# A decode step of attention and a gated MLP: fifteen loads of a few bytes behind the last weights

## The chip, the cores and the metric

The kernel runs on one core of a Trainium2 chip. The metric is the time of one execution on the device in microseconds (us). The core's engines are TensorE (PE in the profile, its weight loads PEld), VectorE (DVE), ScalarE (ACT), GpSimd (POOL) and SyncE (SP). Each has its own stream of instructions, and they meet through semaphores. Data moves between the chip's memory (HBM) and the core's SBUF by sixteen DMA engines, which take their work from queues that SP and ScalarE fill.

## The reference

One token is taken through two blocks, and a gate mixes their results.

```python
x = A_x                                        # [1, 1, 1024]
g = sigmoid((x * gate_w).sum(-1))
# A: grouped attention, 32 query heads, 4 key/value heads of 128, 65536 cached keys
q = x @ wq                                     # wq [1024, 4096]
p = softmax(q . k_cache * 128 ** -0.5)         # k_cache, v_cache [1, 4, 65536, 128]
a = (p . v_cache) @ wo                         # wo [4096, 1024]
# B: a gated MLP with a norm in its second half
z = gelu(x @ w_in)                             # w_in [1024, 3584]
b = (z1 * (w_sp * layernorm(z2) + b_sp)) @ w_out
out = g * a + (1 - g) * b                      # [1, 1, 1024]
```

All inputs and the output are in bfloat16. Nearly all the work is reading: the two caches and the weights come to 162.01 MB, and each byte is used once.

## The kernel before

The kernel holds one large SBUF tensor, `arena`, which it cuts by hand into named regions (a list of names and sizes, placed one behind the other). The largest is `RING`, five slots into which all large loads go. PSUM holds the scores (`scp`), the attention output (`obt`), a small scratch (`mbt`) and the final sum (`fbt`).

The order of the work is written out by hand at the end of the kernel function. `k_step` handles one block of 16384 keys of one head: four VectorE transposes (L499), each followed by TensorE products into `scp` (the helper `mm`, L261 and L263). Blocks go in pairs. After a pair `score_pair` takes the scores to SBUF, `exp_pair` makes their exponentials on ScalarE, and `pv_piece` multiplies a block of values into `obt`. Block B is worked in between, near the start. At the end come the attention's output weights `wo`: `wo_rows` for its first half, then `wo_piece` (L717) for the third quarter and for the last quarter in three cuts of 5, 2 and 1 chunks (`WO_CUT`), all added up in `fbt`. VectorE copies `fbt` to `orow` (L778), and `store` sends `orow` to the output from SP (L365).

Every operation goes through a small recorder, `R.op` (called `P`), which is told the engine, the keys that the operation reads and those that it writes. From these keys `plan` works out which semaphores an operation waits for, and `emit` writes out each engine's instructions in the order in which they were recorded, the waits ahead of them. A load counts up a semaphore of its own name (`dma=`) by 16 when it has landed. At the very end SP waits until the store has landed (L122).

All large loads stand in a list, `stream`, in the order in which they are to be issued, and all leave from SP's queue. `issue` (L386) records as many of them as it can: it stops at the first load whose place in the ring still holds data that isn't marked as used. `done(key)` marks a block as used and calls `issue` again. So the loads' order on SP is that of `stream`, and each waits for the engine that frees its place. The last five are the pieces of `wo`: 4 MB, 2 MB, and the cuts of 1280, 512 and 256 KB. Behind them SP has only the store. Four small loads at the start (`small`, L288) leave from ScalarE's queue: two of eight rows of 256 bytes, two of one element of 2 bytes.

Of the kernel before, what the change touches and what calls it, by code (L numbers as in the profile page):

```python
# [138 lines left out]
def bass_gated_mix__gqa_block_cached__mixer_gmlp__decode_kernel(  # L139
# [23 lines left out]
    FC = FH // 128  # L163
# [12 lines left out]
    QW = DO // NW  # L176
# [11 lines left out]
    def region(name, nbf):  # L188
        nonlocal cur
        OFF[name] = cur  # L190
        cur += (nbf + 15) // 16 * 16

    for name, n in [
        ("M16", 32), ("MQ", 32),
        ("RING", NSUB * SUB), ("KT", NKT * 4096), ("SC", NSC * 2048), ("PSB", 2 * 1024), ("PTSB", 2 * 1024),
        ("QPAD", 4 * QP), ("IDB", 128), ("BM", 256), ("SEL", 16 * 32),
        ("XT", KC), ("WB", 2), ("WBB", 4), ("ONEB", 128),
        ("MAXC", 2 * total), ("LP", 2 * total), ("COLS", 2 * 64), ("DM", 64), ("ONES", 256), ("QALL", 128), ("OVZ", 32 * OC + 31), ("E4Z", 128), ("MHALF", 4),
        ("YB", FC), ("OROW", QW),
    ]:  # L200
        region(name, n)
    NA = (cur + 63) // 64 * 64
# [2 lines left out]
    def ab(name, n, o=0):  # L205
        return arena[:, OFF[name] + o:OFF[name] + o + n]
# [4 lines left out]
    def vw(base, off, dims, p0=0, np_=128):  # L211
        ps = base.ap[0][0]
        return bass.AP(tensor=base.tensor, offset=base.offset + off + p0 * ps,
                       ap=[[ps, np_]] + [list(d) for d in dims])
# [7 lines left out]
    yb, ovz, orow = ab("YB", FC), ab("OVZ", 32 * OC + 31), ab("OROW", QW)  # L222
# [33 lines left out]
    P = R.op  # L256
# [45 lines left out]
    stream = []  # L302
# [58 lines left out]

    osrc = orow[W0:W0 + NW, :]

    def store():
        P("SP", lambda e: e.dma_start(out[0, 0].rearrange("(q n) -> q n", n=QW), osrc), r=["orow"],  # L365
          w=["out"], dma="out")

    issued = [0]
    used = set()
# [2 lines left out]
    def grains(off, w):  # L372
        return list(range(off // GRAN, (off + w + GRAN - 1) // GRAN))

    def issue():

        while issued[0] < len(stream):
            n = issued[0]
            keys, off, src = stream[n]
            w = src.shape[1]  # L380
            gr = grains(off, w)
            if any(k not in used for x in gr if x in owner for k in owner[x]):
                return
            for j, x in enumerate(gr):
                owner[x] = (keys[j * len(keys) // len(gr)],)
            P("SP", lambda e, o=OFF["RING"] + off, w=w, src=src: e.dma_start(arena[:, o:o + w], src),  # L386
              w=[("slot", x) for x in gr], dma="s%d" % gr[0])
            issued[0] += 1

    def use(key):  # L390
        n, off, w = place[key]
        assert n < issued[0], key
        return arena[:, OFF["RING"] + off:OFF["RING"] + off + w], [("slot", x) for x in grains(off, w)]

    def done(key):
        used.add(key)
        issue()

    issue()


# [8 lines left out]
      r=["m32"], w=["sel"])  # L410
    P("DVE", lambda e: e.tensor_reduce(mq, vw(idf, 0, [[1, 16], [16, 8]]), AXX, ALU.add), r=["idf"], w=["mq"])
    P("DVE", lambda e: e.tensor_reduce(mhalf, vw(idf, 0, [[32, 2], [64, 2], [1, 32]]), mybir.AxisListType.XY, ALU.add),
      r=["idf"], w=["mhalf"])
# [4 lines left out]
    for fe in range(4):  # L418
        P("POOL", lambda e, fe=fe: e.tensor_copy(vw(sele, 128 * fe, [[32, 4], [1, 32]]),
                                                vw(idb, 64 * (fe // 2) + fe % 2, [[0, 4], [2, 32]])),  # L420
          r=["idb"], w=[KSE])
# [5 lines left out]
    def f(e):  # L427
        for c in range(KC):
            ins = e.matmul(tb[:, c:c + 1], vw(xm, c, [[8, 128]], 0, 8), oneb[0:8, 0:1], start=(c == 0),  # L429
                           stop=(c == KC - 1), skip_group_check=True)  # L430
        return ins
# [3 lines left out]
      r=["oneb", "wsp", "bsp"], w=["mb"])  # L435
# [6 lines left out]
      r=["ones", "gs"], w=[KTB])  # L442
# [4 lines left out]
      r=["g"], w=["omg"])  # L447
# [328 lines left out]
    for c0, c1 in WO_CUT:  # L776
        wo_piece(3, c0, c1)
    P("DVE", lambda e: e.tensor_copy(orow[0:W0 + NW, :], fb[0:W0 + NW, 0:QW]), w=["orow", "fb"])  # L778
    store()

    R.ahead = 2
# [30 lines left out]
```

## Time and profile before

| what | value |
|---|---|
| time, median of 3 runs | 380.72 us (380.72 to 380.83) |
| span of the profiled execution, first to last instruction | 379.6 us |
| read from HBM | 162.01 MB, 427 GB/s over the span |
| DMA queue q1 (SP's loads and the store) | 3616 packets, 98.9% of sixteen engines |
| DMA queue q10 (ScalarE's small loads) | 36 packets |
| DMA queue q8 (instructions) | 9 packets, 0.15 MB |
| PE busy | 229.6 us (60%) |
| DVE busy | 204.7 us (54%) |
| ACT busy | 23.3 us (6%) |

The profile describes one execution. Its span runs from the first to the last instruction, and all moments in it are counted from the span's start. The three timed runs measure a little more than the span, since they hold what lies around it; the page gives no other time for the profiled execution. "Idle before" and waits name what released an engine, inferred from semaphores. The trace also holds every packet of the DMA engines with its start, its duration, its size and its queue, but not the number of the engine that carried it. A DMA engine's row of packets can be followed where one packet begins as the one before it ends.

### The profile page before, as it was taken

What the parts mean: (1) busy time and instruction counts of PE and PEld (TensorE: products, weight loads), DVE (VectorE), ACT (ScalarE), POOL (GpSimd) and SP (SyncE); (2) the same over time, 40 slices, a digit from 0 to 9 for tenths busy, and PEclk for the clock granted to TensorE, in tenths of its full rate; (3) what the DMA queues carried; (4) which work ended last, traced back from release to release, by engine and by line L of the source; (5) the groups of instructions that cost most, each with busy time, mean ns of one, the idle gap of its engine ahead of it and who ended that gap; (6) DMA issues with size and microseconds to landing.
All of it is one profiled execution on the core that took longest, in us unless ns stands there. A gap on an engine that the chain in (4) does not pass through costs nothing.

```text
span 379.6 us, 2565 instructions
## 1 busy us (share of the span) xinstructions
PE 229.6 (60%) x1444; PEld 57.4 (15%) x835; DVE 204.7 (54%) x162; ACT 23.3 (6%) x24; POOL 8.2 (2%) x36
## 2 busy tenths in 40 slices
PE   0061488458558923895389428952896199737296
PEld 0010011011111200122012001220111011211024
DVE  4011496778389524974597248745773387412021
ACT  1000000010420000002200000022000000220000
POOL 5000000000000000000000000000000000000000
PEclk9997599696859985998599859995799589958599
DMA  9999999999999999999999999999999999999996
GB/s 442 421 414 394 483 388 439 439 453 391 437 442 442 442 430 435 435 442 442 442 430 394 421 442 442 444 435 428 435 435 437 435 442 442 430 421 414 418 428 263
DMA packets 3662, 162.17 MB, mean 427 GB/s; under 512 B 452, under 2 KB 452, under 8 KB 708
## 3 DMA queue, kind: packets, MB, share of 16 engines
q1 hardware_dynamic: 3616, 162.01, 98.9%
q8 instruction: 9, 0.15, 0.1%
q10 hardware_dynamic: 36, 0.00, 0.0%
q14 instruction: 1, 0.01, 0.0%
HBM read 162.01 MB, written 0.00 MB: 427 GB/s over the span
## 4 chain that ended last, share of the span: by engine, by line
DMA 68%; PE 16%; DVE 14%; ACT 1%; issue 1%; ACTq 0%; SPq 0%
DMA arena<-in_A_k_cache_dram 47%; DVE arena L499 12%; DMA arena<-in_A_wo_dram 8%; DMA arena<-in_A_v_cache_dram 7%; PE scp L261 6%; PE scp L263 5%; DMA arena<-in_B_b_sp_dram 5%; PE obt L261 2%; PE obt L263 2%; DVE arena L536 1%; PE fbt L717 1%; ACT arena L531 1%; ACTq L288 0%; PE fbt L665 0%; ACT arena L661 0%
## 5 line engine op out<-in xcount | busy, mean ns | idle before, releaser
L499 DVE STREAM_TRANSPOSE arena<-arena 128x2048 f32<-128x2048 f32 x64 | 143.0, 2284 | 56.7 <-DMA arena<-in_A_k_cache_dram 41.8
L261 PE MATMUL scp<-arena 128*128 128x512 bf16 (+1 forms) x274 | 111.5, 423 | 95.7 <-DVE arena L499 95.4
L263 PE MATMUL scp<-arena 128*128 128x512 bf16 (+1 forms) x275 | 110.4, 418 | 0.0
L261 PE MATMUL obt<-arena 128*64 128x512 bf16 (+2 forms) x334 | 61.4, 410 | 14.2 <-DMA arena<-in_A_v_cache_dram 14.2
L263 PE MATMUL obt<-arena 128*64 128x512 bf16 (+2 forms) x334 | 61.0, 408 | 0.0
L261 PEld LDWEIGHTS scp<-arena 128*128 128x128 bf16 (+1 forms) x274 | 27.4, 104 | 206.6 <-issue 103.5
L536 DVE STREAM_TRANSPOSE arena<-arena 128x2048 bf16<-128x2048 bf16 x7 | 16.2, 2311 | 27.0 <-PE obt L263 24.8
L531 ACT ACTIVATE arena<-arena 128x2048 bf16<-128x2048 f32 x8 | 16.0, 2002 | 218.4 <-DVE arena L528 195.0
L261 PEld LDWEIGHTS obt<-arena 128*64 128x64 bf16 (+1 forms) x334 | 17.9, 111 | 65.7 <-issue 59.0
L516 DVE TENSOR_SCALAR_CACHE_REDUCE arena<-scp 128x2048 f32<-128x2048 f32 x8 | 18.3, 2291 | 16.0 <-PE scp L263 16.0
L565 DVE RECIPROCAL arena<-mbt 128x1 f32<-128x1 f32 x4 | 0.6, 139 | 17.5 <-PE mbt L560 17.5
L539 DVE STREAM_TRANSPOSE arena<-arena 128x1024 bf16<-128x1024 bf16 x2 | 2.5, 1245 | 12.9 <-PE obt L263 12.9
L487 POOL COPY arena<-arena 32x32 bf16<-32x32 bf16 x16 | 3.2, 203 | 234.4 <-PE scp L263 209.8
L434 PE MATMUL mbt<-arena 1*128 1x2 bf16 x1 | 0.2, 159 | 12.2 <-DMA arena<-in_B_b_sp_dram 12.2
L436 DVE COPY arena<-mbt 128x2 f32<-128x2 f32 x1 | 0.2, 159 | 12.2 <-PE mbt L434 12.2
L578 PE MATMUL mbt<-arena 128*64 128x128 bf16 x8 | 1.3, 313 | 7.7 <-DVE arena L572 7.7
L429 PE MATMUL scp<-arena 8*128 8x1 bf16 x8 | 0.7, 198 | 8.6 <-DVE arena L424 8.6
L717 PE MATMUL fbt<-arena 128*32 128x128 bf16 x128 | 4.1, 220 | 1.2 <-DMA arena<-in_A_wo_dram 1.2
L778 DVE CAST arena<-fbt 36x128 bf16<-36x128 f32 x1 | 0.3, 282 | 7.2 <-PE fbt L717 7.2
L528 DVE TENSOR_REDUCE arena<-mbt 128x1 f32<-128x32 f32 x4 | 0.8, 192 | 6.0 <-PE mbt L525 6.0
L717 PEld LDWEIGHTS fbt<-arena 128*32 128x32 bf16 x128 | 3.6, 97 | 2.4 <-issue 1.2
L464 DVE CAST arena<-obt 97x1024 bf16<-97x1024 f32 x1 | 1.2, 1225 | 4.8 <-PE obt L263 4.8
(92 smaller groups left out, 54.9 us busy)
## 6 DMA issues: line engine op xcount, KB each, us to landing
arena<-in_A_k_cache_dram SPq DMA_DIRECT2D x2, 4096.0 KB, 33.3
arena<-in_B_w_in_dram SPq DMA_DIRECT2D x1, 7168.0 KB, 30.5
arena<-in_A_wo_dram SPq DMA_DIRECT2D x1, 4096.0 KB, 38.3
arena<-in_B_w_out_dram SPq DMA_DIRECT2D x1, 3584.0 KB, 21.4
arena<-in_A_wo_dram SPq DMA_DIRECT2D x1, 2048.0 KB, 27.2
arena<-in_A_wo_dram SPq DMA_DIRECT2D x1, 1280.0 KB, 29.9
arena<-in_A_wo_dram SPq DMA_DIRECT2D x1, 512.0 KB, 30.7
arena<-in_A_wo_dram SPq DMA_DIRECT2D x1, 256.0 KB, 30.8
```

The costliest lines, as they stand in the source:

```text
L261: return e.matmul(*a, **kw)
L263: one = e.matmul(*a, **kw).ins
L464: P("DVE", lambda e: e.tensor_copy(psb[0:97, :], ob[0:97, :]), w=["psb", "ob"])
L487: P("POOL", lambda e, pb=pb: e.tensor_copy(vw(qpad, 24 + 32 * pb, [[QP, 4], [1, 8]], 32 * pb, 32), vw(qall, 8 * g, [[32, 4], [1, 8]], 32 * ...
L499: P("DVE", lambda e: e.transpose(ktb(i).bitcast(F32), sl[:, 4096 * p:4096 * (p + 1)].bitcast(F32)), r=keys[4 * p:4 * p + 4], w=[("kt", i % ...
L516: P("DVE", lambda e: e.tensor_scalar(scs(j), scp[:, :], 0.0, None, op0=ALU.add, op1=ALU.max, accum_out=maxc[:, j:j + 1]), w=[("sc", j % 2) ...
L528: P("DVE", lambda e: e.tensor_reduce(gcol(g, K_NB), mb[:, 0:32], AXX, ALU.min), w=[("nb", g), "mb"])
L531: P("ACT", lambda e: e.activation(psb2, scs(j), ACTF.Exp, bias=gcol(j // 2, K_NB), scale=SCALE, accum_out=lp[:, j:j + 1]), r=[("sc", j % 2 ...
L536: P("DVE", lambda e: e.transpose(ptsb2, psb2), r=["psb"], w=[("ptsb", 0), ("ptsb", 1)])
L539: P("DVE", lambda e: e.transpose(ptsb(n), ab("PSB", 1024, 1024 * (n % 2))), r=["psb"], w=[("ptsb", n % 2)])
L578: ins = e.matmul(mb[64 * g:64 * (g + 1), 0:128], vw(sel, 128 * c, [[2, 64]]), osc[:, 128 * c:128 * (c + 1)], start=(c == 0), stop=(c == 3) ...
L717: ins = e.matmul(fb[32 * b:32 * (b + 1), 0:QW], ovz[:, z:z + 32], sl[:, o:o + QW], start=False, stop=(i == 3 and c == 7), tile_position=(0 ...
```

## The change

A region `TINY` of 32 elements is added behind all others in the arena. A new function `marks` records fifteen loads on SP. The load for k (from 15 down to 1) takes k rows of two bfloat16 elements, four bytes, from the first rows of `A_wq` to as many partitions of `TINY`; each load has columns of its own. All fifteen count up one semaphore, `tiny`. `issue` calls `marks` once, right behind the last load of `stream`, which is the 256 KB cut of `wo`. The store now also names the fifteen loads among what it reads, so SP waits for their count as well before it issues the store. Nothing reads the loaded bytes.

```diff
-        ("YB", FC), ("OROW", QW),
+        ("YB", FC), ("OROW", QW), ("TINY", 32),
...
+    tiny = ab("TINY", 32)
+
+    def marks():
+        for k in range(15, 0, -1):
+            def f(e, k=k):
+                with nc.allow_non_contiguous_dma(reason="a few bytes"):
+                    return e.dma_start(tiny[0:k, 2 * k:2 * k + 2], A_wq[0:k, 2 * k:2 * k + 2])
+            P("SP", f, w=[("tiny", k)], dma="tiny")
+
     def store():
-        P("SP", lambda e: e.dma_start(out[0, 0].rearrange("(q n) -> q n", n=QW), osrc), r=["orow"],
-          w=["out"], dma="out")
+        P("SP", lambda e: e.dma_start(out[0, 0].rearrange("(q n) -> q n", n=QW), osrc),
+          r=["orow"] + [("tiny", k) for k in range(1, 16)], w=["out"], dma="out")
...
             issued[0] += 1
+            if issued[0] == len(stream):
+                marks()
```

## The prediction

> **What bounds the kernel now.** I read the page's 40 slices first (DMA at 9 tenths or more in all but the last), then its queue table (the load queue q1 holds 98.9% of sixteen DMA engines), then the last 35 us, where the change sits. The chain of waits ends like this (start us, us, what):
>
> ```profile
> 345.42 0.33 SPq L386
> 345.75 0.04 issue
> 345.79 29.93 DMA arena<-in_A_wo_dram
> 375.72 0.14 issue
> 375.86 2.16 PE fbt L717 x64
> 378.01 0.02 issue
> 378.04 0.28 DVE arena L778
> ```
>
> The reader is to see that the end is set by output weights arriving, then by four short steps. What SP does meanwhile is in its own timeline from 345 us on and in its waits:
>
> ```profile
> 345.42 1.76 SPq L386 DMA_DIRECT2D arena<-in_A_wo_dram  x4
> 378.35 0.37 SPq L365 DMA_DIRECT2D out_dram<-arena  x1
> ```
>
> ```profile
> SPq L365 <- DVE arena L778: 31.1, 1, 31.1
> SPq L386 <- PE obt L263: 14.5, 1, 14.5
> SPq L122 <- DMA out_dram<-arena: 0.8, 1, 0.8
> ```
>
> SP has issued its last weights at 347.19 (345.42 + 1.76) and then has nothing to do for 31.1 us. Last, the tail cut into stretches (us, busy and count of each engine, clock, DMA share, GB/s):
>
> ```profile
> 370.00:375.50 5.50, 4.33 (x88) 2.69 (x81) 0.68 (x2) 0.78 (x1) 0.00 (x0) 1.00 0.98 409
> 375.50:376.40 0.90, 0.54 (x20) 0.57 (x22) 0.00 (x0) 0.00 (x0) 0.00 (x0) 1.00 0.58 232
> 376.40:377.30 0.90, 0.90 (x40) 0.89 (x35) 0.00 (x0) 0.00 (x0) 0.00 (x0) 1.00 0.44 148
> 377.30:378.40 1.10, 0.70 (x20) 0.37 (x14) 0.28 (x1) 0.00 (x0) 0.00 (x0) 1.00 0.00 0
> ```
>
> Two things carry the forecast. The DMA engines don't finish together: their share falls from 0.98 to 0.58 to 0.44. And from 377.30 to 378.40 they move nothing, while TensorE, VectorE and SP bring the result to the store.
>
> The trace's packet records sharpen this. The last load (256 KB) is eight 2 KB packets on each of sixteen engines, 80 ns apart, then a 4-byte packet for the count. The sixteen engines end it between 375.50 and 377.26; seven by 375.87, nine from 376.43 on. The last count packet is over at 377.27, the weight load that waited for it starts at 377.59: **a count takes 0.32 us to be seen**. The store shows the same: its last count packet is over at 379.23, SP's wait passes at 379.57, so 0.34.
>
> **The change, part by part.** Nothing is removed or moved: on every engine but SP the built program has the same instructions in the same order. Added are fifteen loads on SP behind the last weights, and one more count to wait for ahead of the store.
>
> *SP's issuing.* The nearest rows are the four small loads on ScalarE's queue (0.57, 0.28, 0.27, 0.41 us) and SP's own issues (0.33 to 0.44, one of 1.44), with gaps of 0.04. I take 0.44, the row just ahead on the same queue: 15 x 0.48 = 7.2 us, from 347.19 to 354.4. With the shortest row it is 15 x 0.31 = 4.7 (351.9), with the longest 15 x 1.48 = 22.2 (369.4). All of it lies in SP's 31.1 us wait. Nothing is queued behind it except the store, needed at 378.35, and even the longest case is done 6 us before the first DMA engine is through with its weights (375.50). Cost 0. If the queue would not hold so many pending loads, SP would stand still in the same idle time; at 347.19 it already held five whole loads and most of a sixth, and those issues took 0.33 to 0.44.
>
> *The DMA engines.* Each engine meets its short packets after its weights, so no weight can be late by them, as long as they don't disturb engines still on weights. They don't compete visibly: 2 KB packets are 80 ns apart on the engines that end first, with all sixteen busy, and on the one that ends last, with few busy. What a short load costs the engine that carries it: behind 64 KB packets of the first load, the 2-byte data packets of the one-row loads and the 4-byte count packets each delay the next packet by 5 to 6 ns, a 256-byte row by 14. Data and count are 11 ns by these, 24 at most (18 for a recorded 256-byte packet, and 6). The eight-row loads at the start put one row on each of eight engines. If no load gives one engine more than one row, no engine gets more than 15 pairs: 15 x 11 = 0.17 us, at most 15 x 24 = 0.36. Even on the slowest engine they are through by 377.44 to 377.63, and seen 0.34 later, at 377.8 to 378.0. The store can't leave before VectorE ends at 378.32. **0.3 to 0.5 us of cover is left; cost 0.**
>
> Where the cover ends: 378.32 - 0.34 - 377.27 = 0.71 us for 15 pairs, so 47 ns a pair on the slowest engine. The one-row loads ran on one of the eight engines that took the eight-row ones. Following that engine packet by packet (each begins where the one before ends), I get its last weights at 375.65: 2.33 us of cover, 155 ns a pair. Tracks could be exchanged where they cross, so I keep 47 ns as the strict bound. If all 120 rows went to the slowest engine: 120 x 11 = 1.32 us, seen at 378.93, cost 0.6.
>
> Which engines they are is told only by the Trainium skill, DMA: Bandwidth & Descriptors, "Why a DMA increments its semaphore by 16 and not by 1": a load of k rows goes to the lowest-numbered k engines. By that rule one engine gets all fifteen and the last none; the eight packets of each eight-row load agree, and no run here numbers the engines.
>
> *The added wait.* The built program has SP wait for the loads' count first, then for VectorE. SP's separate wait at the end takes 17 ns, and this one is passed before 378.32. Cost 0; met after VectorE instead, 0.02.
>
> *Memory.* 64 bytes per partition behind everything else; no other offset moves.
>
> Sum: span 379.59 + 0. The span lies 1.13 below the median of the three runs (380.72 - 379.59), and I add that again for what lies around it: **380.7 us**.
>
> **The rivals.**
>
> *Each short load waits for the one before it (slower).* No row shows short packets straight behind one another on one engine. If a load's data had to wait until the count before it was seen, each would cost 0.34: 15 x 0.34 = 5.1 us. From 375.65 that ends at 380.75, from 377.27 at 382.37; the store leaves 2.4 to 4.0 us late: **383.1 to 384.7**. It decides from 47 ns a pair (strict bound) or 155 (the followed engine). For it: only the last store waits, so nothing else would hide it. Against it: all through the trace a count packet is followed by the next load's data after 6 ns, and in the store the count packets start 12 to 18 ns behind the data. Chance 0.12.
>
> The Trainium skill speaks for this rival: the same page, "Anatomy of one DMA", gives a DMA about 2.0 us that don't shrink with its size, most of it the receipt of the write. Fifteen of these in a row would be an estimated 30 us and some 409 in all; all side by side, the count would be seen near 379.3 and the time would be some 381.7. The trace disagrees for a store of eight rows: 0.86 us from the end of its issue (378.72) to the wait passed (379.57).
>
> *A tenth instruction fetch (slower).* The instruction queue shows nine fetches of 16 KB. Eight come before 377, and each costs its DMA engine about 1.4 us: 0.95 for itself, and the 64 KB packet beside it takes 2.9 instead of 2.42. That is about the distance between the early and the late engines. One more, on a late engine, would move the end from 377.27 to 378.7: **382.1**. For it: SP's program grows by fifteen instructions and a wait. Against: the fetches come some 45 us apart, as TensorE works through its 2,279 recorded instructions, and SP has some 40. Chance 0.03.
>
> By the Trainium skill, Runtime: NRT & Kernel Launch, "Instruction fetch mechanics", a block of 16 KiB holds 256 instructions; nine times that is 2,304, which fits TensorE's count, and SP's program is far from filling one.
>
> *The end comes earlier (faster).* The only opening is the uneven end of the engines: were the fetches dealt to other engines by the shifted issue times, the last could end with the eighth-last (376.75), -0.5: 380.2. A gain over 0.2% would need all engines level. Nothing in the change moves a fetch before 347. Chance 0.04 for more than 0.2%.
>
> *The change doesn't do what it says.* It would, if the loads left SP only after the weights had landed. Even the longest issue row (369.4) rules that out, and the time would be the same; it counts with the forecast.
>
> **How the numbers follow.** A measurement of this kernel can tell about 0.2% (0.76 us) from no change. Forecast (cover holds, or is missed by less than 0.76): 0.81. Series: 0.12. Tenth fetch: 0.03. Faster: 0.04. So slower 0.15, same 0.81, faster 0.04. The range reaches from 380.2 (fetches dealt luckily) over 381.3 (all rows on the slowest engine) to 382.1 (a tenth fetch); the series rival lies outside.
>
> **What would show it.** After the change, SP's timeline should show fifteen issues from 347.2 to about 354, and its wait for VectorE at L778 should still end last before the store. The packet records should show the 4-byte packets of an engine 5 to 25 ns apart right behind its 2 KB packets, the last by about 377.6; the stretch between last weights and store should stay near 1.1 us; the instruction queue should count nine fetches. I am wrong if the store is released by a DMA instead of VectorE, if the short packets stand 50 ns or more apart, or if the last weights land later than 377.3 against the span's start.

## The result, and the profile after

| | before | after |
|---|---|---|
| median of 6 runs | 380.72 us (380.6 to 380.83) | 381.91 us (381.79 to 382.23) |
| span of the profiled execution | 379.6 us | 380.4 us |

The ratio is 1.0031 (95% interval 1.002 to 1.0042): 1.19 us slower, 0.31%. The time lies inside the predicted range, but the forecast was no change, and this is a change.

The chain of waits of the kernel after (start us, us, what) ends as before, with the output weights, TensorE and VectorE:

```profile
344.94 0.33 SPq L395
345.27 0.04 issue
345.31 30.20 DMA arena<-in_A_wo_dram
375.51 0.14 issue
375.65 1.75 PE fbt L728 x56
377.40 0.01 issue
377.41 0.42 PE fbt L728 x8
377.83 0.02 issue
377.85 0.28 DVE arena L789
```

VectorE is done at 378.13, 0.18 us earlier than before. The chain view stops there and doesn't show the loss. SP's timeline does, and its waits give the releaser (total, times, longest):

```profile
344.94 1.76 SPq L395 DMA_DIRECT2D arena<-in_A_wo_dram  x4
346.75 13.85 SPq L370 DMA_DIRECT2D arena<-in_A_wq_dram  x15
379.20 0.29 SPq L374 DMA_DIRECT2D out_dram<-arena  x1
```

```profile
...
SPq L108 <- DMA arena<-in_A_wq_dram: 18.5, 1, 18.5
SPq L395 <- DVE arena L638: 13.6, 1, 13.6
SPq L808 <- PEq L808: 1.0, 1, 1.0
SPq L122 <- DMA out_dram<-arena: 0.9, 1, 0.9
```

The store leaves at 379.20, 1.07 us behind VectorE; before, the distance was 0.03. The wait for L778 (now L789) that closed SP's idle time is gone from the list. In its place stands a wait for the short loads (L108). The same stretches of the tail as before (us, busy and count by engine, clock, DMA share, GB/s):

```profile
370.00:375.50 5.50, 3.96 (x83) 2.69 (x81) 0.61 (x2) 0.65 (x1) 0.00 (x0) 1.00 0.96 396
375.50:376.40 0.90, 0.75 (x28) 0.79 (x30) 0.00 (x0) 0.00 (x0) 0.00 (x0) 1.00 0.60 223
376.40:377.30 0.90, 0.90 (x36) 0.82 (x30) 0.00 (x0) 0.00 (x0) 0.00 (x0) 1.00 0.38 107
377.30:378.40 1.10, 0.50 (x12) 0.23 (x8) 0.28 (x1) 0.00 (x0) 0.00 (x0) 1.00 0.00 0
378.40:379.60 1.20, 0.00 (x0) 0.00 (x0) 0.00 (x0) 0.00 (x0) 0.00 (x0) 1.00 0.00 0
```

From 377.30 until the store's own packets (379.97) no packet is on record. The last weights end at 377.03, and the last packet of a short load begins at 377.08. Packets of four bytes stand 6 ns apart behind an engine's weights, as predicted. Yet SP waits until 379.12.

Besides packets, the trace records when a count is seen. There the short loads look different. Their 120 counts are seen from 375.88 to 379.12, those of several engines mixed. One even row runs to the end among them: 378.118, 378.319, 378.520, 378.721, 378.922, 379.124. That looks like one engine's row, 0.201 us apart, and the first experiment bears it out. **An engine's packets record a short load every 12 ns, but its counts are seen 0.18 to 0.20 us apart.**

### The profile page after: what moved, and what is told of

Read it like the earlier page. It is cut to its first block, busy times and chain, and to the rows that moved or that the text cites. A ratio compares the mean times of both kernels' runs of the same rounds, so it can differ in the third digit from the quotient of the medians.

```text
span 380.4 us, 2579 instructions
## 1 busy us (share of the span) xinstructions
PE 225.3 (59%) x1442; PEld 56.8 (15%) x835; DVE 204.4 (54%) x162; ACT 23.2 (6%) x24; POOL 8.2 (2%) x36
## 4 chain that ended last, share of the span: by engine, by line
DMA 75%; DVE 12%; PE 12%; issue 0%; ACTq 0%; SPq 0%
DMA arena<-in_A_k_cache_dram 55%; DVE arena L510 11%; DMA arena<-in_A_wo_dram 8%; DMA arena<-in_A_v_cache_dram 7%; DMA arena<-in_B_b_sp_dram 5%; PE scp L261 4%; PE scp L263 4%; PE obt L261 2%; PE obt L263 1%; PE fbt L728 1%; ACTq L288 0%; SPq L395 0%; PE scp L452 0%; DVE arena L451 0%; DVE arena L789 0%
## 5 line engine op out<-in xcount | busy, mean ns | idle before, releaser
L261 PE MATMUL scp<-arena 128*128 128x512 bf16 (+1 forms) x272 | 108.9, 417 | 98.8 <-DVE arena L510 98.3
L263 PE MATMUL scp<-arena 128*128 128x512 bf16 (+1 forms) x275 | 108.7, 412 | 0.2 <-issue 0.2
L261 PE MATMUL obt<-arena 128*64 128x512 bf16 (+2 forms) x334 | 60.8, 406 | 15.1 <-DMA arena<-in_A_v_cache_dram 15.1
L263 PE MATMUL obt<-arena 128*64 128x512 bf16 (+2 forms) x334 | 60.3, 402 | 0.0
L789 DVE CAST arena<-fbt 36x128 bf16<-36x128 f32 x1 | 0.3, 282 | 7.2 <-PE fbt L728 7.2
```

Source lines behind the costliest of these rows:

```text
L261: return e.matmul(*a, **kw)
L263: one = e.matmul(*a, **kw).ins
```

## The experiments

Theory A: on one DMA engine a load's count comes 0.18 to 0.20 us behind the count before it. Its rivals: the 120 counts hold each other up on the one semaphore (B); short pieces of four bytes are dear (C); the loss is not in the wait at all. Each run was timed beside the kernel before on the same chip. Each difference in us below is between the medians of runs taken together, the ratios have 95% intervals.

**Own counts.**

```diff
-            P("SP", f, w=[("tiny", k)], dma="tiny")
+            P("SP", f, w=[("tiny", k)], dma="tiny%d" % k)
```

> The fifteen loads as in the change, but each counts up a semaphore of its own. In the changed kernel the last count packet is recorded at 377.09 us and the last count is seen at 379.12, and counts of one engine come about 0.18 to 0.20 us apart. Theory A (series on the engine: an engine's next short load is not counted until the count before it is through, 0.18 to 0.20 each, up to fifteen on one engine): nothing changes, last count near 379.1, 381.9 us. Theory B (120 counts meet on one semaphore and hold each other up): the spread goes away, last count near 377.5, 380.7 us. Fifteen own semaphores also name each count's load, so each engine's row of counts can be read off.

Measured: 382.1, ratio 1.0035 (1.0022 to 1.0047). B falls, since the rows of counts stay as they were. The trace of the change spoke against B too: six counts there are seen 8 to 9 ns apart on the one semaphore (378.064 to 378.105). And each count now has a name. The load of one row counts on one engine; that engine carries all fifteen loads. Its weights' count is seen at 375.61 and its fifteenth short count at 378.316: 15 x 0.180. The last count of all belongs to the load of six rows (378.991) and has no successor in the loads of fewer rows. So it is on an engine with ten loads, whose weights' count is seen at 377.03: 10 x 0.196. **Not the engine with the most loads ends last, but a late one with ten.** The store left at 379.35, 0.36 behind that count, because SP still went through the remaining waits, two semaphores at a time, 0.06 us apart. That part of 382.1 is the experiment's own.

**One load with fifteen pieces.**

```diff
-        for k in range(15, 0, -1):
...
+                return e.dma_start(vw(tiny, 0, [[4, 15], [1, 2]], 0, 16),
+                                   A_wq[0:16, 0:60].rearrange("p (a b) -> p a b", b=4)[:, :, 0:2])
```

> One load in place of fifteen: sixteen rows of fifteen separate pieces of four bytes, so each of the sixteen engines carries fifteen short data packets and one count (240 pieces in place of 120 rows, 16 counts in place of 120). Theory A (the price is per count in series): one more count per engine, seen about 0.2 us behind the last weights' count (377.4 to 377.6), well before VectorE is done: 380.7 us. Theory C (the price is per piece of four bytes, a short write, whatever is counted): 15 x 0.18 to 0.20 on every engine, the slowest of them too, so the last count is near 380.2, the store about 2 us late: 382.7 us.

Measured: 380.73, ratio 0.9999 (0.9991 to 1.0008). SP's timeline and waits:

```profile
344.68 1.75 SPq L394 DMA_DIRECT2D arena<-in_A_wo_dram  x4
346.47 0.43 SPq L369 DMA_DIRECT2D arena<-in_A_wq_dram  x1
378.13 0.36 SPq L373 DMA_DIRECT2D out_dram<-arena  x1
```

```profile
SPq L108 <- DMA arena<-in_A_wq_dram: 30.6, 1, 30.6
...
SPq L373 <- DVE arena L788: 0.6, 1, 0.6
```

The wait for the short load is over 0.6 us before VectorE's, which closes the idle time again. All sixteen engines carried fifteen pieces, twice as many as in the change, and their counts came 0.16 to 0.22 us behind their weights' counts (both taken in order of time), the last at 377.49. So pieces are cheap and C falls. Counts are dear.

**Rows of 512 bytes.**

```diff
-                    return e.dma_start(tiny[0:k, 2 * k:2 * k + 2], A_wq[0:k, 2 * k:2 * k + 2])
+            P("SP", lambda e, k=k: e.dma_start(ab("SC", 256, 256 * k)[0:k, :], A_wq[0:k, 256 * k:256 * k + 256]),
+              w=[("tiny", k)] + ([("sc", 0), ("sc", 1)] if k == 15 else []), dma="tiny")
```

> The fifteen loads with rows of 512 bytes in place of 4, into a part of the arena that is free by then; SP first waits for ScalarE, which was done with it 10 us before. Theory A: the same row of counts, with 14 to 20 ns more per row: up to fifteen x 0.02 = 0.3 us later, 381.9 to 382.2 us. Theory C (short writes are dear): rows of 512 bytes are cheap, last count by 377.9, 380.7 us.

Measured: 382.19, ratio 1.0038 (1.0024 to 1.0052). The row of counts that ends last is 378.406, 378.607, 378.809, 379.010, 379.211: 0.201 apart, as with four bytes. The row's bytes are not added to the step; they pass inside it.

**Waiting behind the store.**

```diff
-          r=["orow"] + [("tiny", k) for k in range(1, 16)], w=["out"], dma="out")
+          r=["orow"], w=["out"], dma="out")
...
         nc.sync.wait_ge(dsem["out"], final["out"])
+        nc.sync.wait_ge(dsem["tiny"], final["tiny"])
```

> The fifteen loads as in the change, but SP waits for them only behind its wait for the store, not ahead of the store. The store leaves right after VectorE (about 0.03 us). If the wait alone carries the loss and the queues behind it are free: 380.7 to 380.8 us. If the engine that takes all fifteen is itself held until its last count (379.1), its row of the store comes no earlier than that, and the store is through near 379.7 to 379.9: 380.8 to 381.1 us. If the loss came from somewhere else than the wait ahead of the store, it stays at 381.9.

Measured: 381.16, ratio 1.0008 (1.0 to 1.0017), 0.40 us over before. The store leaves at 378.06, 0.03 behind VectorE, as before the change. Most of the loss is therefore the wait ahead of it. Part of the rest shows in the store's eight counts: seven are seen by 379.24, the eighth at 379.432, 0.201 behind the last short load's (379.231). The store's row on that engine stands in the same line: the store's data packets are all over by 378.91. The profiled execution is one of the fastest of this kernel (380.77, against the median of 381.16), so it is not shown that these 0.2 us make up the whole 0.40.

**How many, and where.** Three kernels, in this order: only the five loads of 15 to 11 rows; fifteen loads of sixteen rows; fifteen loads of one row.

```diff
-        for k in range(15, 0, -1):
+        for k in range(15, 10, -1):
...
-          r=["orow"] + [("tiny", k) for k in range(1, 16)], w=["out"], dma="out")
+          r=["orow"] + [("tiny", k) for k in range(11, 16)], w=["out"], dma="out")
```

```diff
-                    return e.dma_start(tiny[0:k, 2 * k:2 * k + 2], A_wq[0:k, 2 * k:2 * k + 2])
+                    return e.dma_start(tiny[0:16, 2 * k:2 * k + 2], A_wq[0:16, 2 * k:2 * k + 2])
```

```diff
-                    return e.dma_start(tiny[0:k, 2 * k:2 * k + 2], A_wq[0:k, 2 * k:2 * k + 2])
+                    return e.dma_start(tiny[0:1, 2 * k:2 * k + 2], A_wq[0:1, 2 * k:2 * k + 2])
```

> Only the five loads of 15 to 11 rows. By theory A the last count is that of an engine that ends its weights late (count seen near 377.1 to 377.4 in the changed kernel) and carries five: plus 5 x 0.20 = 378.1 to 378.4; with 0.08 to the store against VectorE's 378.16 that is 0.0 to 0.3 us late: 380.7 to 381.0 us. If the loss came with having such loads at all, however many, it stays at 381.9.

> Fifteen loads of sixteen rows each, so that every engine carries fifteen, the one that ends its weights last too. Theory A: its weights' count is seen at 377.3 to 377.5, plus 15 x 0.18 to 0.20 = 2.7 to 3.0, so the last count comes at 380.0 to 380.5 and the store 1.9 to 2.4 us late: 382.6 to 383.1 us. If the sum of all counts mattered (225 + 15 in place of 120 at 27 ns each): the spread doubles from 3.2 to 6.5 us, 385 us.

> Fifteen loads of one row each. In the runs with own counts the load of one row counts on the engine that all fifteen loads have in common, and that engine ends its weights early (count seen at 375.6). Theory A: 375.6 + 15 x 0.18 = 378.3, in another run of the fetches up to 375.9 + 15 x 0.2 = 378.9; the store is 0.2 to 0.7 us late: 380.9 to 381.4 us. If the price were per load of SP's queue, whichever engine carries it: 381.9.

Measured, with the moments of each profiled execution (distances are taken before rounding):

| loads | last short count | VectorE done | store leaves | behind VectorE | time, over before | ratio |
|---|---|---|---|---|---|---|
| the change, 15 to 1 rows | 379.12 | 378.13 | 379.20 | 1.07 | 381.91, 1.19 | 1.0031 (1.002 to 1.0042) |
| five, 15 to 11 rows | 378.15 | 378.18 | 378.23 | 0.04 | 380.82, 0.11 | 1.0004 (0.9995 to 1.0012) |
| fifteen, 16 rows | 380.87 | 378.13 | 380.95 | 2.82 | 383.33, 2.62 | 1.0068 (1.0055 to 1.0081) |
| fifteen, 1 row | 378.51 | 378.11 | 378.59 | 0.47 | 381.09, 0.38 | 1.0010 (1.0001 to 1.0019) |

The loss follows the store's delay each time. With sixteen rows the latest weights' count is 377.36, and the last short count stands 3.51 behind it, more than the 2.7 to 3.0 expected, though the row that ends last has steps of 0.178 (380.333, 380.511, 380.689, 380.866). Followed back in steps of 0.17 to 0.18, its fifteen counts begin at 378.41, 1.05 us behind the latest weights' count, so the step alone doesn't explain the whole distance. An instruction fetch begins at 377.23 and lasts 2.19 us (the one at 372.05 took 0.93, the last one of the kernel before 1.48); whether it ran on that engine is not recorded, so this stays open. The sum of counts doesn't set the time: 240 counts at the change's 27 ns each would have taken 6.5 us, and they took 5.1 (375.80 to 380.87). The one-row run is the cleanest. A single engine carries everything, and its counts are seen at 375.975, 376.155, 376.335 and so on to 378.508, thirteen of the fourteen steps 0.180 or 0.181 and one 0.192. SP's own issues took as long there as in the change:

```profile
346.97 13.73 SPq L370 DMA_DIRECT2D arena<-in_A_wq_dram  x15
378.59 0.29 SPq L374 DMA_DIRECT2D out_dram<-arena  x1
```

So the price is not per load of SP's queue either.

**Ahead of the weights.** Does only the counting lag, or does the engine stand still?

```diff
-            if issued[0] == len(stream):
-                marks()
...
+            if n == len(stream) - 5:
+                marks()
```

> The same fifteen loads and the same wait, but the loads are issued ahead of the first piece of the output weights instead of behind the last, so that 8 MB of weights stand behind them on the engines. Theory A1 (only the counts of an engine come 0.18 to 0.20 us apart, its data flows on meanwhile): the fifteen counts are through some 10 us before the end, the last weights land as before (near 377.3), nothing is late: 380.7 us. Theory A2 (the engine stands still until each count is through): engine 0 loses 15 x 0.18 = 2.7 us and a late engine with ten loads 10 x 0.2 = 2.0 us of its transfer time, the last weights come 1.7 to 2.0 us later: 382.4 to 382.7 us.

Measured: 382.05, ratio 1.0038 (1.0025 to 1.0051). The short loads are through at 360.37, 19 us before the store, and the run is still 1.34 slower. One stretch of this run, and below it the same stretch of the change:

```profile
355.00:360.00 5.00, 1.83 (x10) 0.59 (x6) 0.00 (x0) 0.00 (x0) 0.00 (x0) 0.50 0.81 282
```

```profile
355.00:360.00 5.00, 1.91 (x10) 0.58 (x6) 0.00 (x0) 0.00 (x0) 0.00 (x0) 0.50 0.91 393
```

The rate there falls from 393 GB/s (419 in the kernel before) to 282. That SP issues the first piece of `wo` 6 us later (335.24 instead of 328.94) is not the reason: its first packet begins at 355.98, and at 355.90 in the change. The four-byte packets are again recorded 6 ns apart, but the first 32 KB packet behind them lasts up to 2.44 us instead of 1.21. The last weights end at 378.68 instead of 377.03 (377.26 in the kernel before), and the loss arrives through the weights:

```profile
345.17 32.02 DMA arena<-in_A_wo_dram
377.19 0.14 issue
377.33 2.18 PE fbt L728 x64
379.51 0.02 issue
379.53 0.28 DVE arena L789
```

Theory A1 (data flows on meanwhile) falls. Fifteen short loads in a row hold the engine. The size comes out below A2: 1.4 to 1.7 us in this execution, which is one of the slower ones (382.38), against 1.7 to 2.0, and a median of 382.05 against 382.4 to 382.7.

**Spread out, and on the other queue.**

```diff
-    def marks():
-        for k in range(15, 0, -1):
+    def marks(k0=15, k1=0):
+        for k in range(k0, k1, -1):
...
-            if issued[0] == len(stream):
-                marks()
+            if 3 <= issued[0] < 18:
+                marks(18 - issued[0], 17 - issued[0])
```

> The same fifteen loads on SP's queue, but one behind each of fifteen large loads from the third on, instead of all at one place. The run ahead of the weights showed that fifteen in a row hold the engine: the first 32 KB packet behind them lasted up to 2.4 us instead of 1.21, and the last weights came 1.4 to 1.7 us late. Theory H1 (each count holds its engine 0.18 to 0.20 us, wherever it stands): an engine that carries ten loses 2.0, one that carries fifteen 2.7, and the end comes 1.4 to 2.0 us later: 382.1 to 382.7 us. Theory H2 (an engine reads on while one count is pending, and only several in a row stop it): a single one is hidden in the large packets around it: 380.7 to 380.9 us.

```diff
-            P("SP", f, w=[("tiny", k)], dma="tiny")
+            P("ACT", f, w=[("tiny", k)], dma="tiny")
```

> The fifteen loads as in the change, issued by ScalarE instead of SP, from about 337 us on, when it has nothing else to do for 32 us. The four small loads at the start of the kernel show how the two queues share an engine: one packet from one, one from the other, so data and count of a short load each follow one large packet (2.42 us for 64 KB, 0.61 for 16 KB). Thirty packets are through by about 375, ahead of the last weights. H1 (each count holds the engine 0.18 to 0.20): 1.4 to 2.0 us late, 382.1 to 382.7 us. H2 (hidden between large packets): 380.7 to 380.9 us.

Measured: spread 381.24, ratio 1.0012 (1.0003 to 1.0021), 0.56 over before; other queue 380.9, ratio 1.0004 (0.9995 to 1.0013), 0.22 over. Spread out, the last weights end at 377.52, 0.26 us later than before; on the other queue at 376.97, and the last short count is seen at 372.22. H1 (every count holds its engine 0.18 to 0.20) falls in both. H2 fits the other queue and comes out low for the spread loads: between large packets most of the price is hidden, not all. What the 0.56 us of the spread loads is made of stays open; the 0.22 us of the other queue can't be told from no change.

## Why the prediction was wrong, point by point

That 381.91 lies inside the range is luck. The range reached up to 382.1 only for a tenth instruction fetch, which did not come, and the rival that came closest to the mechanism stood outside it. Of the three signs of being wrong that the prediction named, one came: a DMA's count releases the store, not VectorE.

- **SP's issuing: no cost, as predicted, though longer.** 13.85 us instead of 7.2, inside the bounds of 4.7 and 22.2. The first ten took 0.30 to 0.48 each and the last five 1.07 to 2.63. That fits a queue that would not hold so many loads, which the prediction had considered, and it cost nothing, as the working said. With one row and with sixteen rows a load the eleventh is again the first long one (1.01 and 1.57 us), so the sum of rows is not what fills it.
- **The weights: undisturbed, as predicted.** They end at 377.03, against 377.26 before.
- **The price of a pair: the step that failed.** "Data and count are 11 ns by these, 24 at most." The 5 to 6 ns were taken from how little a short packet delays the record of the next packet, behind 64 KB packets. The packets after the change stand 6 ns apart too, so the row was read rightly, but for the wrong quantity. SP waits for counts, and those come 0.18 to 0.20 us apart. The term of 15 x 11 ns = 0.17 us, at most 0.36, was in fact 2.7 us on the engine with all fifteen (15 x 0.180) and 2.0 on the one that ended last (10 x 0.201). The prediction had noted that no row shows short packets straight behind one another, and its upper bound still came from packets alone; the 0.32 us until a count is seen belonged into that bound, not only into a rival.
- **Where the cover ends: right, and it decided.** 47 ns a pair on the slowest engine, 155 on the one that carries all fifteen. Measured 180 exceeds both. For the engine with all fifteen, 15 x 0.18 = 2.7 against 2.33 us of cover leaves 0.37 us, and the run with one row lost 0.38. So close a match is partly chance, since in that run's own profile the store was 0.47 us behind VectorE. In the change a late engine with ten loads (ten as in the run with own counts) overtook it: 377.1 + 10 x 0.201 = 379.1.
- **The series rival: the mechanism, at half its price.** It took 0.34 a load and 15 loads (383.1 to 384.7). The runs show 0.18 to 0.20 and ten loads on the engine that ends last. Its contrary evidence, a count packet followed by data after 6 ns, was again taken from packet records, which don't show the hold: ahead of the weights, packets recorded 6 ns apart went with 2.44 us in place of 1.21 for the next large one.
- **The 2.0 us by the Trainium skill** (DMA: Bandwidth & Descriptors, "Anatomy of one DMA"). That section is written for DMAs that GpSimd issues, and these are issued by SP. The estimate from it with all loads side by side (some 381.7) lies near the 381.91 measured, but not by its mechanism: a fixed price would not have gone with five loads (0.11 us) nor risen with sixteen rows (2.62 us).
- **The lowest-numbered engines.** The own counts agree with the rule that the prediction took from the Trainium skill (same page, "Why a DMA increments its semaphore by 16 and not by 1"): the loads have 15, 14, 13 and so on to 1 counts, and the engine that has the one-row load's count has one of each. No run numbers the engines.
- **The tenth fetch** did not come: the instruction queue counts nine in both. **The added wait** cost 0.08 us from the last count to the store's issue, where the prediction had 0.02 for a wait met after VectorE.

The Trainium skill, DMA: Bandwidth & Descriptors, "Queues, rings and completion order", says that a count lands only after every earlier write of its engine. The series agrees with that order; the section gives no time for it. What an engine does in the 0.18 us was not tried and stays open; no run separates the count from the write just ahead of it.

## What to carry to other kernels

The price of short loads in a row at the end of a kernel is the step from count to count on an engine, in these runs 0.18 to 0.20 us a load, and not the few nanoseconds that their packets take: one load of fifteen pieces was free where fifteen loads cost 1.2 us. Where several small loads stand behind one another, make them one, or put them where large packets of another queue pass between them. When the chain of waits ends in the same engine as before and the time has still grown, look at what the waiting queue itself names, and read when counts are seen, not when packets are recorded.

## What the runs showed of the hardware that was not expected

- Packets of four bytes are recorded 6 ns apart while their counts are seen 0.180 us apart (one engine, one-row run) or 0.201 (another, in the change and with 512 bytes).
- Fifteen short loads in a row ahead of weights hold the engine: a 32 KB packet of 1.21 us lasted up to 2.44, although the records of the short packets show no pause.
- In the change SP's issue of a short load takes 0.30 to 0.48 us for the first ten, then up to 2.63. With one row and with sixteen rows a load, too, the eleventh is the first long one.
- With fifteen semaphores to wait for, SP takes about 0.06 us for each instruction that holds two waits, also when both counts have long been seen.
